# A gated sum of linear attention and a GEGLU block: all gate/up phases ahead of all down phases, and another opening

## The chip, the cores and the metric

The kernel runs on one core of one Trainium2 chip. The metric is device time in microseconds (us) of one execution; three runs of the kernel before gave 289.71, 290.48 and 290.14, a median of 290.14. Engines are named as the profile names them: PE is TensorE (PEld its weight loads), DVE is VectorE, ACT is ScalarE, POOL is GpSimd, SP is SyncE, which here only issues DMAs.

## The reference, cut to what matters

```python
# x: 2048 tokens x 640, bf16; H = 32 heads of Dh = 20; F = 1728
q, k, v = heads(x @ wqkv)
pq, pk  = q @ w_phi[h], k @ w_phi[h]                        # per head, 20 x 20
phi_q   = concat(softmax(pq), softmax(-pq))                 # 40 features a head
phi_k   = concat(softmax(pk), softmax(-pk))
kv, z   = phi_k.T @ v, phi_k.sum(tokens)                    # per head
a = ((phi_q @ kv) / (phi_q @ z + 1e-6)) @ wo                # linear attention, not causal
b = (gelu(x @ w_gate) * (x @ w_up)) @ w_down                # GEGLU block on the same x
g = sigmoid((x * gate_w).sum(-1))
out = g * a + (1 - g) * b
```

`kv` and `z` are sums over all 2048 tokens, so no attention output can be made before the last token has been through `phi_k`. The block `b` depends on `x` alone.

## The kernel before, in words

The program is written out by hand, in the order in which each engine runs it. A small recorder (`_Sched`, L21) notes for each tile which operation wrote it last and which read it, and puts a semaphore wait ahead of an operation that needs one. There is no reordering: what stands first on an engine or a DMA queue runs first, and a wait holds up all that stands behind it on that engine or queue. Two DMA queues are used, SP's and ACT's. A DMA on ACT's queue is issued by ACT itself, between its other instructions.

The 2048 tokens are 16 tiles of 128 rows (index `t`) or four blocks of 512 (index `b`). The 640 columns of x are 5 pieces of 128 (`kt`).

**The opening** (`loads`, L207, and the first half of `attention_state`, L533). SP issues four loads of one tile of x each (`xtok`, L215), the v columns of `wqkv` in three loads (L218), then transposed loads: x tiles 4 and 5 (L227), the k columns of `wqkv` (L222, `wkT`), x tiles 6 and 7, the q columns (`wqT`), x tiles 8 to 11 and 12 to 15, and after those the weights of the second half. ACT first runs one Exp on a constant (L230), which brings its function table in, later one of the four copies of transposed x (L297), then the issues of `wphi` and of the gate's column (L546, L549). PE runs eight matmuls on constants (L539), transposes the four x tiles of the first block (L291), and computes v for these four tiles, one `kt` at a time over all four (`v_step`, L364), so that each load of v columns is used as it lands.

After that come v of tiles 4 and 5, and the folds (`fold`, L319), which multiply the k and q columns by the block-diagonal `w_phi` (matmuls L332, copied out at L345 or L347), five for k and five for q, one for each `kt`. Between them stand v of tiles 6 and 7 (`v_early`) and phi_k's logits of tiles 0 to 3 (`k_early`, both through L352). In the kernel before, all five k folds stand ahead of v of tile 6:

```python
        f(0, "k", (2, 3), "d")
        ...
        f(4, "k", (2, 3), "d")
        ve(6, 4)
        ke(0, 6)
        ve(7, 0)
        ke(1, 2)
```

The pair of numbers is the pair of PSUM banks that a step writes (there are eight, 0 to 7); the letter says whether DVE ("d") or ACT ("a") copies the result out. The logits of tile 3 are made in two pieces, one ahead of the last q fold and one behind it. `k_norm` (L425 to L434, DVE) makes the softmax of phi_k; `gram` (L450) adds one tile to `kv`; `pq` (L512) makes phi_q's exponentials for one block and one piece, with two Exp on ACT (L519). The first three `pq` stand ahead of the first `gram`; they write banks 7, 6 and 0.

**The middle.** For tiles 4 to 15: v and k logits (`vk`), `k_norm`, `gram`, and the remaining `pq`.

**The second half** (`ffn`, L755). For each of the four blocks there is a gate/up phase (`gateups`: 14 chunks of 128 columns of gate and up; gelu on ACT at L628, product on DVE at L630, into the tile `hT`) and a down phase (`downs`: four tiles in two pairs, `down_pair`, L691). The down matmuls (L713) run as 64-row halves side by side. Each adds the product times `w_down` and the attention output times `wo` in one PSUM group; ACT writes it out with the gate's factor (L726), and SP stores it (L737). The step `num` (L646) makes the attention output of one tile: 20 short matmuls (L656), eleven DVE operations (L672 to L685) and one DMA transpose on SP into `goT` (L688). Two `num` stand in the second gate/up phase; the others stand in the down phases, four in each of the first three and two in the last, each well ahead of the pair that uses it. There are two buffers for the product, `hT0` and `hT1`, so a block's gate/up phase cannot be more than two ahead of its down phase:

```python
        gateups(0, state)
        gateups(1, first_nums)
        for b in range(self.NB):
            downs(b, {at[k]: 4 * b + 2 + k for k in range(4 if b < 3 else 2)})
            if b < 2:
                gateups(b + 2, none)
```

## Time and profile before

| | |
|---|---|
| runs | 289.71, 290.48, 290.14 us, median 290.14 |
| profiled execution | 289.71 us, span 288.5 us |
| granted TensorE clock | 1.0 |
| PE busy | 282.2 us (98%), 3018 matmuls |
| DVE busy | 174.7 us (61%) |
| ACT busy | 104.5 us (36%) |
| DMA | 18.67 MB, mean 65 GB/s |
| opening, up to the first `gram` | 0 to 30.9 us |
| middle | 30.9 to 86.7 us |
| gate/up 0 and 1, down 0 | from 86.7 us; down 0 from 141.0 to 162.8 us |
| gate/up 2, down 1 | 162.8 to 192.0 us, 192.0 to 213.8 us |
| gate/up 3, down 2, down 3 | 213.8 to 243.0 us, 243.0 to 264.8 us, from 264.8 us |

The profiled execution is the fastest of the three runs; 1.2 us of its time lie around its span. Durations below are of this execution. A matmul's duration in a row covers its whole way through the array, so matmuls that follow each other overlap: 128x512 has a mean of 379 ns, while one starts every 0.216 us. A few matmul records are missing in the trace (a count of 49 where the program has 50).

### The profile page before, as it was taken

The numbers are of one execution on the slowest core, as the hardware profiler recorded it, in microseconds if no ns is written. First come the engines' busy times: TensorE is split into PE (matmuls) and PEld (weight loads), VectorE is DVE, ScalarE is ACT, GpSimd is POOL, SyncE is SP. The second block draws the span as 40 slices with busy tenths as digits, with TensorE's granted clock in tenths as the row PEclk, the third lists the DMA queues.
The fourth block names the chain that finished last, engine by engine and source line by source line (L and its number), as shares of the span: only waits on it lengthen the run. The fifth ranks groups of instructions, "written<-read, shape, count | busy, mean of one in ns | idle before, by whom it ended". The sixth has DMA issues, their size and how long they took to land.

```text
span 288.5 us, 7003 instructions
## 1 busy us (share of the span) xinstructions
PE 282.2 (98%) x3018; PEld 186.1 (65%) x3033; DVE 174.7 (61%) x353; ACT 104.5 (36%) x199; POOL 5.3 (2%) x36
## 2 busy tenths in 40 slices
PE   8999899999999999999999999999999999999996
PEld 5566589999994444444577544457754445777785
DVE  2337999999987553468588133258823334884801
ACT  3266787776663232322111332311133222112111
POOL 7000000000000000000000000000000000000000
PEclk9999999999999999999999999999999999999999
DMA  6999997000002000011023300003320000222221
GB/s 187 218 190 224 370 368 206 0 2 2 0 2 48 0 0 0 3 24 23 2 25 67 97 0 0 0 3 25 53 89 22 0 0 2 25 49 70 70 72 48
DMA packets 37193, 18.67 MB, mean 65 GB/s; under 512 B 28970, under 2 KB 36906, under 8 KB 37162
## 3 DMA queue, kind: packets, MB, share of 16 engines
q1 hardware_dynamic: 36496, 18.19, 26.4%
q8 instruction: 24, 0.39, 0.5%
q10 hardware_dynamic: 666, 0.03, 0.2%
q14 instruction: 7, 0.06, 0.1%
HBM read 9.04 MB, written 2.62 MB: 40 GB/s over the span
## 4 chain that ended last, share of the span: by engine, by line
PE 94%; DMA 2%; DVE 1%; issue 1%; SPq 1%; ACT 0%; DVEq 0%
PE ps L352 59%; PE ps L713 28%; PE ps L656 2%; PE ps L450 2%; DMA w<-in_A_wqkv_dram 2%; PE ps L364 2%; PE ps L332 1%; SPq L215 1%; DVE Dk L425 1%; DVE wq L345 0%; DVE Ek L434 0%; DVE Dk L429 0%; SPq L218 0%; ACT outsb L726 0%; PE ps L314 0%
## 5 line engine op out<-in xcount | busy, mean ns | idle before, releaser
L630 DVE TENSOR_TENSOR hT<-ps,gl 128x512 bf16<-128x512 f32 x52 | 35.6, 690 | 64.9 <-PE ps L352 64.8
L713 PE MATMUL ps<-wd_sb,hT 64*128 64x320 bf16 (+2 forms) x918 | 66.2, 288 | 0.0
L352 PE MATMUL ps<-xT,wg_sb 128*128 128x512 bf16 (+1 forms) x265 | 63.8, 379 | 0.6 <-issue 0.5
L352 PE MATMUL ps<-xT,wu_sb 128*128 128x512 bf16 (+1 forms) x263 | 63.3, 379 | 0.5 <-DVE hT L630 0.2
L628 ACT ACTIVATE gl<-ps 128x512 bf16<-128x512 f32 x52 | 30.9, 596 | 70.4 <-PE ps L352 66.0
L713 PEld LDWEIGHTS ps<-wd_sb,hT 64*128 64x128 bf16 x918 | 43.1, 94 | 15.6 <-ACT gl L628 0.8
L352 PEld LDWEIGHTS ps<-xT,wu_sb 128*128 128x128 bf16 (+1 forms) x270 | 26.5, 99 | 29.8 <-DVE hT L630 0.5
L352 PEld LDWEIGHTS ps<-xT,wg_sb 128*128 128x128 bf16 (+1 forms) x270 | 26.0, 99 | 29.1 <-issue 0.5
L726 ACT ACTIVATE outsb<-ps,Gm 128x320 bf16<-128x320 f32 (+2 forms) x31 | 14.5, 515 | 75.6 <-PE ps L713 75.6
L352 PE MATMUL ps<-w,xT 128*64 128x512 bf16 (+6 forms) x398 | 41.4, 325 | 0.1
L352 PEld LDWEIGHTS ps<-w,xT 128*64 128x64 bf16 (+1 forms) x400 | 35.7, 107 | 4.7
L713 PE MATMUL ps<-wo_sb,goT 64*128 64x320 bf16 (+2 forms) x340 | 27.8, 288 | 0.0
L352 PE MATMUL ps<-xT,wq 128*64 128x512 bf16 (+1 forms) x184 | 25.9, 380 | 0.1
L434 DVE TENSOR_TENSOR Ek<-Ek,Dk 128x640 bf16<-128x640 bf16 x32 | 25.0, 822 | 0.6
L683 DVE TENSOR_TENSOR O<-ps,RH 128x640 bf16<-128x640 f32 x32 | 24.8, 816 | 0.0
L425 DVE TENSOR_REDUCE Dk<-Ek 128x64 f32<-128x1280 bf16 x16 | 23.7, 1479 | 0.0
L414 ACT ACTIVATE Ek<-ps 128x640 bf16<-128x640 f32 x32 | 20.7, 703 | 4.2 <-PE ps L352 4.2
L519 ACT ACTIVATE Eq<-ps 128x512 bf16<-128x512 f32 x40 | 21.6, 607 | 1.5 <-PE ps L352 1.2
L713 PEld LDWEIGHTS ps<-wo_sb,goT 64*128 64x128 bf16 x340 | 16.0, 94 | 5.4
L352 PEld LDWEIGHTS ps<-xT,wq 128*64 128x64 bf16 (+1 forms) x185 | 15.3, 109 | 2.9
L406 ACT ACTIVATE vaug<-ps 128x640 bf16<-128x640 f32 x12 | 8.5, 706 | 11.5 <-PE ps L352 11.5
L672 DVE RECIPROCAL RH<-ps 128x32 f32<-128x32 f32 x16 | 5.7, 358 | 7.5 <-PE ps L656 6.8
(65 smaller groups left out, 148.9 us busy)
## 6 DMA issues: line engine op xcount, KB each, us to landing
out_dram<-outsb SPq DMA_DIRECT2D x7, 320.0 KB, 2.3
wd_sb<-in_B_w_down_dram SPq DMA_DIRECT2D x1, 2080.0 KB, 13.3
wg_sb<-in_B_w_gate_dram SPq DMA_DIRECT2D x1, 1120.0 KB, 6.3
wu_sb<-in_B_w_up_dram SPq DMA_DIRECT2D x1, 1120.0 KB, 9.6
wg_sb<-in_B_w_gate_dram SPq DMA_DIRECT2D x1, 960.0 KB, 9.5
wu_sb<-in_B_w_up_dram SPq DMA_DIRECT2D x1, 960.0 KB, 9.8
wo_sb<-in_A_wo_dram SPq DMA_DIRECT2D x1, 800.0 KB, 9.8
xtok<-in_A_x_dram SPq DMA_DIRECT2D x4, 160.0 KB, 2.6
```

Of the source, the lines that this page charges most:

```text
L352: self.sc.op("pe", lambda e: e.matmul(self.ps[a:z, bank * 512 + c0:bank * 512 + c0 + n], lhs[:, a:z], rhs, start=first, stop=fin), reads=r ...
L364: sc.op("pe", lambda e, c0=c0, n=n, bk=bk, col=col: e.matmul(self.bank(bk)[:, col:col + n], self.xT[:, kt, t * P:(t + 1) * P], self.w3[:, ...
L406: self.sc.op("act", lambda e: e.activation(self.vaug[:, sv, :, 0:self.DH], self.bank(B, self.D).rearrange("p (h d) -> p h d", d=self.DH), ...
L414: self.sc.op("act", lambda e, s=s, scale=scale: e.activation(self.Ek[:, se, s, :], self.ps[:, o:o + self.D], AF.Exp, scale=scale), reads=[ ...
L425: sc.op("dve", lambda e: e.tensor_reduce(self.Dk[:, se, 0, :].rearrange("p (s h) -> p s h", h=H), self.Ek[:, se, :, :].rearrange("p s (h d ...
L434: sc.op("dve", lambda e, v=v, r=r: e.tensor_tensor(v, v, r, ALU.mult), reads=[("Rk", se)], writes=[("Ek", se, s)])
L519: sc.op("act", lambda e, s=s, scale=scale: e.activation(self.Eq[:, s, i, b * self.BT:(b + 1) * self.BT], self.bank(bank), AF.Exp, scale=sc ...
L628: sc.op("act", lambda e: e.activation(self.gl[:, slot, :], self.bank(banks[0]), AF.Gelu_apprx_tanh), reads=[("ps", banks[0])], writes=[("g ...
L630: sc.op("dve", lambda e: e.tensor_tensor(hT[:, c, :], self.bank(banks[1]), self.gl[:, slot, :], ALU.mult), reads=[("ps", banks[1]), ("gl", ...
L683: dve(lambda e, o=o, f=f, s=s: e.tensor_tensor(o, V[s][:, :, :, 0:DH], f, ALU.mult), rb + [key(6 + s)], [("O", s, sl)], guard=old)
L713: sc.op("pe", lambda e: e.matmul(self.bank(bk, w), lhs, rhs, start=opens and x == 0, stop=end and not opens, skip_group_check=True), reads ...
L726: sc.op("act", lambda e: e.activation(dst, self.bank(bk, w), AF.Copy, scale=g), reads=rd, writes=wr)
```

## The change: the order of the phases, and another opening

In the second half, a third product buffer `hT2` is added, and the product of block 3 is written over the part of `xT` that holds x of blocks 0 to 2, which by then has been read for the last time. So all four gate/up phases run first, and then the four down phases one after the other. The `num` steps keep their places inside their phases.

In the opening, x of the first block comes in two loads of two tiles each, one on SP's queue and one on ACT's; `wphi` and the gate's column follow on ACT's queue at once. The v columns come in five loads of one `kt` each. The Exp at the head of ACT's program is gone, so its table load stands ahead of its first copy. PE's first matmuls are seven on a tile that DVE sets to zero. The copy of x tile 3 moves from DVE to ACT. v of tile 6 moves ahead of the last three k folds, v of tile 7 behind them and ahead of the first k logits, k logits of tiles 1 and 2 move, those of tile 3 are one piece behind the last q fold, and some of the steps use other banks; the third `pq` writes bank 7 and not bank 0.

```diff
+        self.zero = T("zero", [P, 512], BF16)
+        self.hT2 = T("hT2", [P, NFC, BT], BF16)
...
         def xload(q, j):
-            sc.dma(q, lambda e: e.dma_start(self.xtok[:, j, :], x4[:, j, :]), writes=[("xtok", j)])
...
+            sc.dma(q, lambda e: e.dma_start(self.xtok[:, j:j + 2, :], x4[:, j:j + 2, :]),
+                   writes=[("xtok", j), ("xtok", j + 1)])
...
         sc.op("pool", lambda e: e.memset(self.gz[:, :], 0.0), writes=["gz"])
-        sc.op("act", lambda e: e.activation(self.gtmp[:, 0:1], self.nc.const_aps.tensor(1.0, [P, 1], BF16), AF.Exp),
-              writes=["gtmp"])
-        for j in range(self.TB):
-            xload("sp", j)
-        for a, z in ((0, 1), (1, 3), (3, 5)):
-            vload("sp", a, z)
+        xload("sp", 0)
+        xload("act", 2)
+        sc.dma("act", lambda e: e.dma_start(
+            self.wphi_sb[:, :, :], self.wphi.rearrange("h d f -> (h d) f").rearrange("(i p) f -> p i f", p=P)),
+            writes=["wphi"])
+        for kt in range(KD):
+            sc.dma("sp", lambda e: e.dma_start(self.w3[:, kt, 0:D], w3[:, kt, 2 * D:3 * D]), writes=[("wv", kt)])
+        sc.dma("act", lambda e: e.dma_start(self.gz[0:KD, :], self.gw.rearrange("(k p) -> k p", p=P)), writes=["gz"])
         xturn(4, 2)
-        wload(self.wkT, D, "wkT", 0, 5)
+        wload(self.wkT, D, "wkT")
         xturn(6, 2)
...
-        bank = 6 + n % 2 if bank is None else bank
+        bank = 6 + n % 2
...
-        for n in (512, 512, 512, 512, 512, 512, 128, 128):
-            sc.op("pe", lambda e: e.matmul(self.bank(0, n), ones[:, 0:P], ones[:, 0:n], start=True, stop=True),
-                  writes=[("ps", 0)])
+        sc.op("dve", lambda e: e.memset(self.zero[:, :], 0.0), writes=["zero"])
...
+        warm(7)
         xt(0, 6, "d")
         xt(1, 7, "a")
         xt(2, 2, "d")
-        xt(3, 3, "d")
...
+        xt(3, 3, "a")
...
-        ve(4, 6)
-        ve(5, 0)
+        self.v_early(4, 6)
+        self.v_early(5, 0)
         f(0, "k", (2, 3), "d")
         f(1, "k", (4, 5), "a")
-        f(2, "k", (6, 7), "d")
-        f(3, "k", (0, 1), "a")
-        f(4, "k", (2, 3), "d")
-        ve(6, 4)
-        ke(0, 6)
-        ve(7, 0)
-        ke(1, 2)
+        self.v_early(6, 6)
+        f(2, "k", (2, 3), "d")
+        f(3, "k", (4, 5), "a")
+        f(4, "k", (0, 1), "d")
+        self.v_early(7, 6)
+        self.k_early(0, 2)
         f(0, "q", (4, 5), "d")
         f(1, "q", (6, 7), "d")
-        ke(2, 0)
+        self.k_early(1, 0)
         f(2, "q", (4, 5), "d")
         f(3, "q", (6, 7), "d")
-        self.proj(3, 640, 384, 2, 128, ["wk2"])
+        self.k_early(2, 2)
         f(4, "q", (4, 5), "d")
-        self.proj(3, 1024, 257, 3, 0, ["wk2", "wgate"])
-        self.k_evac(3, 2)
         self.k_norm(0)
+        self.k_early(3, 0)
         self.k_norm(1)
         self.pq(0, 1, 1)
         self.pq(0, 0, 0)
-        self.pq(0, 3, 3, 0)
+        self.pq(0, 3, 3)
...
+    def hT(self, b, c):
+
+        if b == 3:
+            return self.xT[:, c // 3, (c % 3) * self.BT:(c % 3 + 1) * self.BT]
+        return (self.hT0, self.hT1, self.hT2)[b][:, c, :]
...
-        oldw, hT = (self.oldw, self.hT0) if b % 2 == 0 else (self.oldk, self.hT1)
-        hk = b % 2
+        old = (self.oldw, self.oldk, [], [("xT", t) for t in range(12)])[b]
+        hT, hk = self.hT(b, c), b
...
         gateups(0, state)
         gateups(1, first_nums)
+        gateups(2, none)
+        gateups(3, none)
         for b in range(self.NB):
             downs(b, {at[k]: 4 * b + 2 + k for k in range(4 if b < 3 else 2)})
-            if b < 2:
-                gateups(b + 2, none)
```

## The prediction

> **What bounds the kernel now.** I read the busy shares and the chain first, then PE's waits behind the opening, then the opening in order of time.
>
> ```profile
> PE 282.2 (98%) x3018; PEld 186.1 (65%) x3033; DVE 174.7 (61%) x353; ACT 104.5 (36%) x199; POOL 5.3 (2%) x36
> PE 94%; DMA 2%; DVE 1%; issue 1%; SPq 1%; ACT 0%; DVEq 0%
> ```
>
> ```profile
> PE ps L450 <- DVE Ek L434: 0.8, 1, 0.8
> PE ps L352 <- issue: 0.5, 3, 0.2
> PE ps L352 <- DVE hT L630: 0.2, 1, 0.2
> ```
>
> The first fence shows a PE-bound kernel. The second lists every wait of PE from 31 us to 288: the 0.8 at its head is the first gram, and behind it lie 0.7 us. So no phase of the second half waits for a buffer, and a third one has no wait to remove. What can move the time is the opening, and the cost of changing from one kind of matmul to another.
>
> ```profile
> 0.84 2.93 PE L539 MATMUL ps<-const-bfloat16-1.0 128*128 128x512 bf16 x8 [0.84 <-PEq L829]
> 3.56 1.81 PE L291 MATMUL ps<-ident,xtok 128*128 128x128 bf16 x15
> 5.63 0.72 PE L291 MATMUL ps<-ident,xtok 128*128 128x128 bf16 x5 [0.26 <-DMA xtok<-in_A_x_dram]
> 6.14 1.36 PE L364 MATMUL ps<-w,xT 128*128 128x480 bf16 x8
> 7.93 3.45 PE L364 MATMUL ps<-w,xT 128*128 128x480 bf16 x24 [0.43 <-DMA w<-in_A_wqkv_dram]
> 15.09 1.96 PE L332 MATMUL ps<-BD,wkT 128*128 128x140 bf16 x30
> 17.09 5.39 PE L352 MATMUL ps<-w,xT 128*128 128x512 bf16 x39
> 22.32 0.79 PE L332 MATMUL ps<-BD,wqT 128*128 128x140 bf16 x12
> 26.87 3.18 PE L352 MATMUL ps<-xT,wq 128*128 128x512 bf16 x14
> 30.88 0.46 PE L450 MATMUL ps<-Ek,vaug 128*64 128x120 bf16 x11 [0.82 <-DVE Ek L434]
> ```
>
> In the timeline of PE (start, length, group, idle before), PE waits for loads of x and v until 7.93 us, then only at the first gram. That wait ends a DVE series:
>
> ```profile
> 24.90 2.30 DVE L345 CAST wq<-ps 128x640 bf16<-128x640 f32 x3 [0.44 <-PE ps L332]
> 27.12 1.48 DVE L425 TENSOR_REDUCE Dk<-Ek 128x64 f32<-128x1280 bf16 x1
> 28.63 0.55 DVE L429 RECIPROCAL Dk<-Dk 128x64 f32<-128x64 f32 x1
> 29.21 1.56 DVE L434 TENSOR_TENSOR Ek<-Ek,Dk 128x640 bf16<-128x640 bf16 x2
> ```
>
> The transposed loads of x tiles 4 and 5 (issued at 4.13) and tiles 6 and 7 (issued at 11.33) took 6.8 and 5.4 us from issue to landing, in this order:
>
> ```profile
> xT<-in_A_x_dram SPq DMA_TRANSPOSE x1, 6.8
> xT<-in_A_x_dram SPq DMA_TRANSPOSE x1, 5.4
> ```
>
> So tiles 6 and 7 landed at 16.73. Their first use, v of tile 6, began at 16.88 (its shown start, 17.09, less one missing record of 0.216): they were 0.15 us early, by luck of the order.
>
> **The change, part by part.** Parts 1 to 3 lead to the first gram, part 4 is the rest.
>
> *1. First loads.* Both x loads are issued at 0.80 now; before, the fourth was issued at 2.19 and landed 3.4 later, at 5.6. 0.66 MB at the 261 GB/s of the window from 2 to 5 us need 2.5 us; with first packets at about 2.0, x lands at 4.5 at best. At worst it lands at 5.6, as before. I take 5.0, the middle, since nothing shows two queues at once. DVE's memset of zeros is bounded by POOL's 128x128 memset (0.20) and a DVE copy of 128x640 (0.49); seven warm-up matmuls at 0.42 (eight, or 6.5 lengths of 512, filled 0.84 to 3.56) end at about 4.1: hidden under the x loads, and if x came earlier they would cost up to 0.6. ACT issues three DMAs (0.41, 0.43, 0.66) and loads its table (1.28) by 3.7, 2 us ahead of its first copy: nothing, unless x came before 3.5. `wphi` lands earlier, and nothing waited for it on the chain.
>
> The 20 transposes took 0.107 each. The warm-up matmuls of 128x512 have a mean of 626 ns, later ones 379: PE runs at half speed until some 6.4 us, although the granted clock reads 1.0 throughout. From 5.0, 13 transposes fit before 6.4, seven more at half the time end at 6.8. ACT copies x tile 1 and then tile 3 at 0.70 each, where DVE took 0.49, so tile 3 is ready at 7.7; the last v pair (0.27) ends the first `kt` at 8.0, against 7.93 before. Each v load is one `kt` now: the second lands between 6.0 (the first one before) and 7.85 (the double one), so nothing waits. Opening: +0.1, between -0.3 (x at 4.5) and +1.6.
>
> The +1.6 is what stays cold: if half speed lasted until 9.8, the transposes would end at 7.1 and the first `kt` at 9.5. The Trainium skill, "TensorE: Matmul & The Clock Gate", Part 1, says the clock opens after a busy window of about 3.4 us that runs free of the kernel; PE now idles from 4.1 to 5.0, so one more window is possible. By this estimate from the page, the whole sum below would be +0.4 instead of -0.1; no row here shows the window.
>
> *2. v of tile 6, moved ahead of three k folds.* Each fold has six matmuls. The 12 of two q folds filled 22.32 to 22.95: 0.63. So v of tile 6 is reached at 15.09 + 0.63 = 15.72, +0.1: 15.8. The tiles land at 16.73 if nothing changes. SP reaches their issue about 0.5 us earlier (six issues at 0.46 instead of seven), which would give 16.2. But the DMA share is 0.91 to 1.24 in all windows from 2 to 17 us; the engines, not SP, look full, and the bytes ahead are the same. I take 16.73: a new wait of 0.9 us, in which PE does nothing, and which swallows any delay of part 1 below 0.9. Bounds: 16.2, and 18.1 if this load takes the 6.8 of its sister. What queues behind: all of PE. The k and q columns (landed 14.0 and 20.2) stay ahead of their use at 15.2 and 21.8.
>
> *3. From there to the first gram.* A v step or a k step takes 1.36 (four filled 16.88 to 22.32). v6, three k folds (0.95), v7, k0, two q folds (0.63), k1, two q folds, k2, one q fold (0.32): 9.33, then k3: 10.69, two `pq` of 1.08: 12.85. The third `pq` writes bank 7, as the first did, so it waits for ACT: k3's exponentials occupied ACT for 1.23 (26.92 to 28.15) from 0.26 after PE, until 12.2; the first `pq`'s two Exp finish at 13.3. A new wait of 0.5; the third `pq` ends at 14.4. DVE copies the last q fold by 10.3 and needs 3.57 (27.12 to 30.69): 13.9, earlier than PE. So the old 0.82 wait is gone and a bank wait stands there. The first gram starts at 16.73 + 14.4 = 31.15, against 30.88: +0.3. With the bounds of part 2: -0.25 and +1.6. From there every row is PE's again, so this passes to the end.
>
> *4. Order of phases.* PE's work is the same. Two rows show the change from down to gate/up:
>
> ```profile
> 162.98 1.03 PE L352 MATMUL ps<-xT,wg_sb 128*128 128x512 bf16 x4 [0.16 <-issue]
> 214.00 1.03 PE L352 MATMUL ps<-xT,wg_sb 128*128 128x512 bf16 x4 [0.16 <-issue]
> 140.23 0.81 PE L352 MATMUL ps<-xT,wu_sb 128*128 128x512 bf16 x3
> 140.98 0.31 PE L713 MATMUL ps<-wd_sb,hT 64*128 64x320 bf16 x2
> ```
>
> In the last two, three matmuls from 140.23 at 0.216 end their issue at 140.88; the down matmul follows 0.10 later. Two changes each way go: 4 x 0.10 = 0.4. Bounds: 0, if the array drains elsewhere, and 0.5 with the idle column's 0.16. Product writes over `xT` wait for PE's reads of the third phase, past already; if not, one DVE product (0.69). The down phases stand back to back, as down 2 and 3 did: DVE was busy 16.15 of 21.72 us there, and PE did not wait. The transposed attention output of the last `num` has 57 steps of 0.133, plus 14, or 9.4 us, for 0.4 on PE, 4.0 on DVE (a quarter of 16.15) and 2.8 of DMA. On SP each transpose still stands behind the same store. Nothing.
>
> Sum: +0.3 - 0.4 = -0.1 on the profiled 289.71 (span 288.5 and 1.2 around it). That execution is 0.43 below the median, so I forecast 290.0 against 290.14.
>
> **The rivals.**
> *A. Slower: tiles 6 and 7 land later.* ACT's queue now sends `wphi`, 640 short rows, into the v loads, and the sister load took 6.8. Against it: same bytes. Landing at 18.1 instead of 16.73 gives 290.0 + 1.4 = 291.4; it decides from 17.75 on, when the total passes +0.87.
> *B. Faster: loads are bound by SP's issue.* Tiles land 0.5 earlier, and the first gram comes 0.55 earlier than in the sum: 289.5. To pass 0.87 the tiles must be there by 16.0; in full, with x at 4.5, PE reaches tile 6 at 15.4 and finds it: first gram at 29.8, -1.1, with -0.4: 288.6. For it speaks SP's unbroken series of issues; against it the full DMA share.
> *C. The third buffer does nothing at all* (changes cost PE the same elsewhere): +0.3, 290.4. *D. Half speed lasts one window longer:* PE reaches tile 6 at 17.2, 0.5 later than in the sum: 290.5. Both are inside the band below.
>
> **How the numbers follow.** 0.3%, or 0.87 us, is about what a measurement of this kernel can tell from no change. Forecast with C, D and B's milder form: 0.50. A, with any other late load in the opening: 0.36. B in full: 0.14. Range: 289.1 to 291.4; its top is A's price, its lower end lies between B's 289.5 and 288.6, and some 2 in 10 stay outside. The forecast's own range is 289.3 to 290.9.
>
> **What would show it.** Right: an idle time of PE of about 0.9 ahead of v of tile 6, put down to `xT`'s load; about 0.5 ahead of the third `pq`, put down to ACT; none ahead of the first gram, at about 31.2; one change to the down matmuls instead of three, and no new wait of PE behind 31 us. Wrong: tiles 6 and 7 outside 16.2 to 17.7, or a wait inside the run of four down phases.

## The result, and the profile after

The changed kernel takes 288.37 us (median of 6 runs, 287.87 to 289.37), the kernel before beside it 289.74 (6 runs, 289.20 to 290.48). The ratio is 0.9954, with a 95% interval of 0.9933 to 0.9976: 1.3 us or 0.46% faster. The forecast was 290.0, in a range from 289.1 to 291.4. The profiled execution took 288.19 us, its span 286.9.

The page's busy shares and its chain of the changed kernel read almost as before:

```profile
PE 281.2 (98%) x3017; PEld 185.5 (65%) x3032; DVE 174.7 (61%) x353; ACT 105.0 (37%) x199; POOL 5.3 (2%) x36
PE 93%; SPq 3%; DMA 2%; ACT 1%; issue 1%; ACTq 0%
```

PE's work is the same, so the gain lies in when PE could begin it. The waits of PE from 31 us on, of the changed kernel:

```profile
PE ps L352 <- DVE hT L632: 0.2, 1, 0.2
PE ps L352 <- issue: 0.2, 1, 0.2
```

The wait at the first gram is gone, and of three issue waits of 0.5 in all one of 0.2 is left. The opening, in the timeline of PE of the changed kernel (start, length, group, idle before):

```profile
1.24 3.17 PE L541 MATMUL ps<-zero 128*128 128x512 bf16 x7 [1.24 <-DVE zero L537]
4.29 1.29 PE L291 MATMUL ps<-ident,xtok 128*128 128x128 bf16 x20
5.42 4.72 PE L364 MATMUL ps<-w,xT 128*128 128x480 bf16 x32
...
13.84 0.79 PE L332 MATMUL ps<-BD,wkT 128*128 128x140 bf16 x12
14.80 1.53 PE L352 MATMUL ps<-w,xT 128*128 128x512 bf16 x10 [0.18 <-DMA xT<-in_A_x_dram]
16.18 1.11 PE L332 MATMUL ps<-BD,wkT 128*128 128x140 bf16 x18
...
25.90 2.11 PE L352 MATMUL ps<-xT,wq 128*128 128x512 bf16 x9
28.34 1.25 PE L352 MATMUL ps<-xT,wq 128*128 128x512 bf16 x5 [0.34 <-ACT Eq L519]
29.52 0.48 PE L450 MATMUL ps<-Ek,vaug 128*64 128x120 bf16 x11
```

The 20 transposes start at 4.29, all 32 matmuls of the first four `kt` of v follow without a pause (before, the second `kt` began at 7.93), v of tile 6 waits 0.18, and the first gram starts at 29.52 instead of 30.88: 1.36 us earlier. On DVE the softmax is ready ahead of it (27.43 + 1.56 = 28.99):

```profile
25.33 1.47 DVE L425 TENSOR_REDUCE Dk<-Ek 128x64 f32<-128x1280 bf16 x1
27.43 1.56 DVE L434 TENSOR_TENSOR Ek<-Ek,Dk 128x640 bf16<-128x640 bf16 x2
```

Behind the first gram this pair of profiles shows little: up to the first gate/up matmul 49.27 us against 49.24 (it starts at 80.12 in the kernel before, since some gate/up chunks already stand in the middle), from there to PE's last start 205.08 against 205.51 (-0.43), and from that to the end of the span 3.06 against 2.84 (+0.2). The phases are in the order meant, with one change to down matmuls (timeline of PE, changed kernel):

```profile
196.97 1.03 PE L352 MATMUL ps<-xT,wu_sb 128*128 128x512 bf16 x4
197.93 0.31 PE L714 MATMUL ps<-wd_sb,hT 64*128 64x320 bf16 x2
198.07 0.56 PE L658 MATMUL ps<-KV,Eq 64*128 64x88 bf16 x20
```

So in this pair -1.36 belong to the opening. What moved there are the loads. The timeline of SP's queue (issue and how long SP was held by it), of the changed kernel:

```profile
0.79 0.41 SPq L217 DMA_DIRECT2D xtok<-in_A_x_dram  x1
1.27 2.30 SPq L234 DMA_DIRECT2D w<-in_A_wqkv_dram  x5
3.62 1.44 SPq L225 DMA_TRANSPOSE xT<-in_A_x_dram  x1
5.10 4.58 SPq L221 DMA_TRANSPOSE wkT<-in_A_wqkv_dram  x1
9.72 1.41 SPq L225 DMA_TRANSPOSE xT<-in_A_x_dram  x1
```

and of the kernel before:

```profile
0.80 1.83 SPq L215 DMA_DIRECT2D xtok<-in_A_x_dram  x4
2.67 1.42 SPq L218 DMA_DIRECT2D w<-in_A_wqkv_dram  x3
4.13 2.25 SPq L227 DMA_TRANSPOSE xT<-in_A_x_dram  x1
6.43 4.87 SPq L222 DMA_TRANSPOSE wkT<-in_A_wqkv_dram  x1
11.33 1.40 SPq L227 DMA_TRANSPOSE xT<-in_A_x_dram  x1
```

x tiles 6 and 7 are issued at 9.72 instead of 11.33 and land 5.0 later instead of 5.4,

```profile
xT<-in_A_x_dram SPq DMA_TRANSPOSE x1, 5.0
```

that is at 14.72 instead of 16.73. Of these 2.01 us, 0.51 is the earlier start of the first transposed load (3.62, 4.13), 0.81 and 0.29 are that the two transposed loads ahead hold SP for 1.44 and 4.58 instead of 2.25 and 4.87, and 0.4 is the landing. In the window from 2 to 5 us (length, busy time and count of PE, PEld, DVE, ACT and POOL, granted clock, DMA share, GB/s) the kernel before shows

```profile
2.00:5.00 3.00, 3.00 (x20) 2.03 (x19) 0.49 (x1) 0.41 (x3) 2.29 (x15) 1.00 0.91 261
```

and the changed kernel

```profile
2.00:5.00 3.00, 3.00 (x19) 1.32 (x18) 0.22 (x1) 1.28 (x1) 2.29 (x15) 1.00 1.03 324
```

A share of 0.91 stood beside 261 GB/s, one of 1.03 beside 324: the share of 0.91 was no ceiling.

### The profile page after: what moved, and what is told of

Read it like the earlier page. It is cut to its first block, busy times and chain, and to the rows that moved or that the text cites. A ratio compares the mean times of both kernels' runs of the same rounds, so it can differ in the third digit from the quotient of the medians.

```text
span 286.9 us, 7006 instructions
## 1 busy us (share of the span) xinstructions
PE 281.2 (98%) x3017; PEld 185.5 (65%) x3032; DVE 174.7 (61%) x353; ACT 105.0 (37%) x199; POOL 5.3 (2%) x36
## 4 chain that ended last, share of the span: by engine, by line
PE 93%; SPq 3%; DMA 2%; ACT 1%; issue 1%; ACTq 0%
PE ps L352 60%; PE ps L714 28%; PE ps L658 2%; DMA xT<-in_A_x_dram 2%; PE ps L450 2%; SPq L221 2%; PE ps L332 1%; SPq L234 1%; SPq L225 1%; ACT Ek L414 0%; ACT Eq L519 0%; SPq L217 0%; ACT outsb L727 0%; ACT gcol L417 0%; ACTq L42 0%
## 5 line engine op out<-in xcount | busy, mean ns | idle before, releaser
L632 DVE TENSOR_TENSOR hT<-ps,gl 128x512 bf16<-128x512 f32 x39 | 26.7, 690 | 38.6 <-PE ps L352 38.5
L714 PE MATMUL ps<-wd_sb,hT 64*128 64x320 bf16 x648 | 49.5, 296 | 0.0
L352 PEld LDWEIGHTS ps<-xT,wu_sb 128*128 128x128 bf16 (+1 forms) x270 | 26.5, 99 | 29.8 <-DVE hT L632 0.5
L714 PEld LDWEIGHTS ps<-wd_sb,hT 64*128 64x128 bf16 x648 | 31.0, 94 | 12.1 <-issue 0.4
L632 DVE TENSOR_TENSOR xT<-ps,gl 128x512 bf16<-128x512 f32 x13 | 9.0, 691 | 18.2 <-PE ps L352 18.2
L714 PE MATMUL ps<-wd_sb,xT 64*128 64x320 bf16 (+2 forms) x270 | 16.7, 269 | 0.0
```

Source lines behind the costliest of these rows:

```text
L352: self.sc.op("pe", lambda e: e.matmul(self.ps[a:z, bank * 512 + c0:bank * 512 + c0 + n], lhs[:, a:z], rhs, start=first, stop=fin), reads=r ...
L632: sc.op("dve", lambda e: e.tensor_tensor(hT, self.bank(banks[1]), self.gl[:, slot, :], ALU.mult), reads=[("ps", banks[1]), ("gl", slot)], ...
L714: sc.op("pe", lambda e: e.matmul(self.bank(bk, w), lhs, rhs, start=opens and x == 0, stop=end and not opens, skip_group_check=True), reads ...
```

## The experiments

Each is told by its edit to the kernel before or to the changed kernel. Kernels of one group ran on one chip, with runs of the kernel before on that chip. Its medians lie between 289.66 and 290.82, so only ratios and differences within a group are compared. A word on single profiles: the same kernel's first gram differs between executions (29.52 and 30.31 in two profiles of the changed kernel), so the profiles carry places and waits, and the runs carry the time.

### First group: the change taken apart (kernel before: 289.66)

**The order of phases alone**, on the kernel before:

```diff
+        self.hT2 = T("hT2", [P, NFC, BT], BF16)
...
         gateups(1, first_nums)
+        gateups(2, none)
+        gateups(3, none)
         for b in range(self.NB):
             downs(b, {at[k]: 4 * b + 2 + k for k in range(4 if b < 3 else 2)})
-            if b < 2:
-                gateups(b + 2, none)
```

> The kernel before with only the third product buffer and the new order of the phases. Theory 1 (the opening made most of the gain, the order of phases the predicted 0.4): 0.4 us faster than before, first gram at 30.9 as before, one change from gate/up to down matmuls instead of three. Theory 2 (the order of phases made the gain): 1.2 us or more faster. Rival (nothing comes of it): within 0.1.

Measured: 289.49, ratio 0.999 (0.9978 to 1.0002), about 0.3 us at the ratio. The runs alone do not tell it from nothing. The profiles do: from the start of the first gram to the end of the span, the nine profiles here that have the new order of phases show 256.90 to 257.42, mean 257.16; the eleven that have the old one show 257.20 to 257.80, mean 257.55. The order of phases is worth 0.39. From the first gate/up matmul to PE's last start, which leaves out both ends, the two sets don't even touch: 204.91 to 205.08 with the new order, 205.34 to 205.51 with the old one.

**The changed kernel with the old order of phases**, the same edit the other way:

```diff
-        gateups(2, none)
-        gateups(3, none)
         for b in range(self.NB):
             downs(b, {at[k]: 4 * b + 2 + k for k in range(4 if b < 3 else 2)})
+            if b < 2:
+                gateups(b + 2, none)
```

> The changed kernel with the second half put back to the old order (two buffers in use). Theory 1: about 1.0 us faster than before, first gram at 29.5; with the 0.4 of the phases this gives the whole. Theory 2: within 0.2 of before.

Measured: 288.65, ratio 0.9963 (0.9949 to 0.9977), -1.0 by medians; first gram at 29.42. The opening carries the gain of the first gram whole, and the two halves (-0.3 and -1.07 at their ratios) add up to the change.

**The loads alone**, on the kernel before, with its order of folds and steps:

```diff
-        for j in range(self.TB):
-            xload("sp", j)
-        for a, z in ((0, 1), (1, 3), (3, 5)):
+        xload("sp", 0)                       # two tiles each
+        xload("act", 2)
+        ...                                  # wphi and the gate's column on ACT's queue
+        for a, z in ((0, 1), (1, 2), (2, 3), (3, 4), (4, 5)):
             vload("sp", a, z)
```

The Exp on a constant is left out of this one as well.

> The kernel before with only the loads of the opening changed: x in two loads on two queues, w_phi and the gate's column on ACT's queue behind it, v columns in five loads, no Exp ahead; PE's order and warm-up stay. Theory 1a (the loads carry the opening's gain): x on hand at about 4.3, v of tile 6 about 1.2 us earlier than 16.88 without a wait, 0.8 to 1.2 us faster than before. Theory 1b (the order of the folds carries it, the loads only feed it): less than 0.4, since the DVE series ahead of the first gram stays.

Measured: median 288.94, ratio 0.9987 (0.9962 to 1.0012). The interval is wide because the executions fall into two bands: eight from 288.43 to 289.04, four from 290.85 to 291.33. The profile is of the lower band (timeline of PE, loads alone):

```profile
4.29 1.29 PE L294 MATMUL ps<-ident,xtok 128*128 128x128 bf16 x20 [0.52 <-DMA xtok<-in_A_x_dram]
5.42 4.67 PE L367 MATMUL ps<-w,xT 128*128 128x480 bf16 x32
29.57 0.46 PE L453 MATMUL ps<-Ek,vaug 128*64 128x120 bf16 x11 [0.82 <-DVE Ek L437]
```

With the old folds, and with the old wait of 0.82 still there, the first gram comes at 29.57. In the lower band (median 288.71, 0.95 faster) the loads give nearly the whole gain of the opening; the new order of folds and steps adds 0.05 to the first gram (29.52).

**The new order of folds and steps alone**, with their banks, on the kernel before:

```diff
-        f(2, "k", (6, 7), "d")
-        f(3, "k", (0, 1), "a")
-        f(4, "k", (2, 3), "d")
-        ve(6, 4)
+        self.v_early(6, 6)
+        f(2, "k", (2, 3), "d")
+        f(3, "k", (4, 5), "a")
+        f(4, "k", (0, 1), "d")
...
-        self.pq(0, 3, 3, 0)
+        self.pq(0, 3, 3)
```

> The kernel before with only the new order of folds, v and k steps and their banks; loads stay. By the prediction's parts 2 and 3: tiles 6 and 7 land at 16.7, PE waits 0.9 for them, first gram at 31.15, 0.3 us slower than before. Theory 1b: faster by 0.4 or more.

Measured: 290.37, ratio 1.0023 (1.0008 to 1.0038), 0.7 us slower. Timeline of PE, folds alone:

```profile
14.84 0.79 PE L332 MATMUL ps<-BD,wkT 128*128 128x140 bf16 x12
16.48 1.53 PE L352 MATMUL ps<-w,xT 128*128 128x512 bf16 x10 [0.85 <-DMA xT<-in_A_x_dram]
...
29.91 1.25 PE L352 MATMUL ps<-xT,wq 128*128 128x512 bf16 x5 [0.34 <-ACT Eq L519]
31.10 0.49 PE L450 MATMUL ps<-Ek,vaug 128*64 128x120 bf16 x11
```

This is the picture that the prediction drew for the whole change: 0.85 ahead of v of tile 6 (forecast 0.9), 0.34 ahead of the third `pq` (0.5), no wait at the first gram, which comes at 31.10 (31.15). With the old loads its parts 2 and 3 hold.

### Second group: what of the loads (kernel before: 290.82)

**Both x loads on SP**, in the loads-alone kernel:

```diff
-        xload("act", 2)
+        xload("sp", 2)
```

> The loads-only kernel with both x pairs on SP's queue. Theory 1a' (longer rows carry the gain): x as early as with two queues or up to 0.5 later (second issue at 1.26), span within 0.4 of the loads-only kernel's 287.2. Theory 1a'' (the second queue carries it): x at 5 or later, span near the 288.5 of before.

Measured: 289.41, ratio 0.9955 (0.9937 to 0.9972). x lands in two steps (transposes from 3.71, the second half at about 5.0), the first `kt` of v waits 0.61, the second starts at 7.46, and the window from 2 to 5 us moves 292 GB/s. With the first gram at 30.39 the profile looks as if the second queue were needed, but the runs don't bear that out: they are 1.3 us faster at the ratio, as the changed kernel's were, and within 0.2 of the two-queue kernel with the longer warm-up below, on the same chip. Two double loads hold SP for 0.88 us, four single ones for 1.83, two on two queues for 0.41; the first halving is enough to keep the gain.

**Four single x loads, two on each queue**, in the loads-alone kernel:

```diff
-        xload("sp", 0)
-        xload("act", 2)
+        for q, js in (("sp", (0, 1)), ("act", (2, 3))):
+            for j in js:
+                xload(q, j)                  # one tile each
```

> The loads-only kernel with four one-tile x loads, two on each queue. Theory 1a' (longer rows): x lands at 5 or later although two queues issue it, 261 GB/s or so between 2 and 5 us. Theory 1a'' (the second queue): x at 4.3 to 4.6 and the rate stays near 324 GB/s.

Measured: 288.90, ratio 0.9937 (0.9915 to 0.9959); the second `kt` at 6.78, 318 GB/s from 2 to 5 us. The loads are as short as in the kernel before, and the rate is nearly that of the changed kernel: longer loads are not needed for it. That the second queue raised it above the 292 of one queue rests on one profile each; SP is held by its x issues for 0.89 here, as with both pairs on one queue.

**A longer warm-up**, eight matmuls of 512 columns, in the loads-alone kernel:

```diff
-        for n in (512, 512, 512, 512, 512, 512, 128, 128):
+        for n in (512,) * 8:
```

> The loads-only kernel with eight full warm-up matmuls, so that PE works until x is there. Theory 3 (a pause of PE ahead of the transposes lets the full speed come a window later in some executions, which makes the loads-only kernel's runs of 290.9 to 291.3): no run over 290, median 288.6, like the opening of the changed kernel. Rival (those runs have another cause, loads that come late): a quarter to a third of the runs stay at 290.9 or more.

Measured: 289.26, ratio 0.9951 (0.9933 to 0.9968); all six executions between 288.74 and 289.75, and PE idles 0.18 ahead of the transposes instead of 0.52. There is no second band, but with a third of the executions in it, six without one come about by chance in 9 of 100 cases ((2/3)^6), and the chip is another.

**The changed kernel with its third `pq` back in bank 0:**

```diff
-        self.pq(0, 3, 3)
+        self.pq(0, 3, 3, 0)
```

> The changed kernel with the third pq in bank 0 again. Theory 4 (the wait of 0.34 us ahead of the third pq is ACT's hold on bank 7 and lies on the path): the wait goes, first gram 0.3 to 0.4 earlier at about 29.1, 0.3 us faster than the changed kernel. Rival: the DVE series ends last then (29.0 in the changed kernel) and leaves less than 0.1.

Measured: 288.04, ratio 0.9906 (0.9885 to 0.9926). From 5 us on the profile shows no wait of PE at all.

### Third group: bank 0 beside the changed kernel, and two single parts (kernel before: 289.99)

The changed kernel itself once more, and the bank-0 form beside it:

> The changed kernel itself, beside the next run on the same chip: 288.2 to 288.8 if this chip is like the first, 1.0 to 1.5 us faster than before.

> The changed kernel with the third pq in bank 0, now beside the changed kernel on one chip. Theory 4: 0.3 us faster than the changed kernel (its wait was 0.34). Rival: within 0.1 of it.

Measured: 288.38, ratio 0.9941 (0.9920 to 0.9961), and 287.74, ratio 0.9915 (0.9894 to 0.9936). The profile of the changed kernel is of its slowest execution here (288.76). In the timeline of PE:

```profile
6.69 4.69 PE L364 MATMUL ps<-w,xT 128*128 128x480 bf16 x32
15.70 1.52 PE L352 MATMUL ps<-w,xT 128*128 128x512 bf16 x10
30.31 0.49 PE L450 MATMUL ps<-Ek,vaug 128*64 128x120 bf16 x11
```

PE comes to v of tile 6 only at 15.70 and does not wait, for tiles 6 and 7, issued at 9.43, landed at 14.2.

By medians bank 0 is 0.64 faster than the changed kernel; by means 0.74, give or take 0.4. The profiles show how much of it is the bank: from the start of v of tile 6 to the first gram it takes 14.60 to 14.72 in the eight profiles that have the new order of steps and the third `pq` in bank 7, and 14.17 in both with bank 0. So the bank is worth about 0.44, a little more than the idle time of 0.34 that it removes; the rest of the 0.64 is within the noise. The timeline of PE of the bank-0 form, where the 0.34 of the changed kernel stood:

```profile
14.59 1.52 PE L352 MATMUL ps<-w,xT 128*128 128x512 bf16 x10
25.35 3.40 PE L352 MATMUL ps<-xT,wq 128*128 128x512 bf16 x15
28.76 0.46 PE L450 MATMUL ps<-Ek,vaug 128*64 128x120 bf16 x11
```

Three `pq` in a row and the gram behind them, with no wait. This is the fastest version: it beats both kernels, 2.25 us ahead of the one before on this chip.

**Only x in two loads on two queues**, on the kernel before, without the Exp; v stays in three loads, `wphi` and the gate's column late:

```diff
-        for j in range(self.TB):
-            xload("sp", j)
+        xload("sp", 0)
+        xload("act", 2)
```

> The kernel before with only x of the first block in two loads on two queues (and without the Exp, which would hold up ACT's issue); v columns in three loads and w_phi late, as before. Theory 1 in its narrowest form (the early x carries the opening's gain): x on hand at about 4.3, 0.7 us or more faster than before. Rival (the v columns in five loads or the early w_phi are needed too): PE waits for v columns up to 7.4 or so, less than 0.4 faster.

Measured: 293.39, ratio 1.0098 (1.0059 to 1.0137), 3 us slower. Timeline of PE, x alone:

```profile
6.55 5.67 PE L363 MATMUL ps<-w,xT 128*128 128x480 bf16 x32
14.28 0.23 PE L313 MATMUL ps<-ident,gz 128*128 128x128 bf16 x1 [2.05 <-DMA gz<-in_gate_w_dram]
```

With SP's issues ahead of time, the transposed load of the k columns is issued at 4.73, and `wphi`, issued on ACT's queue at 5.74, lands only 8.6 us later (4.0 in the changed kernel, where it is issued at 1.24). PE stands 2.05 us ahead of the gate's column, which is issued behind `wphi`, and then the granted clock falls. Windows of the same kernel, columns as above, the granted clock third from the end:

```profile
14.00:15.00 1.00, 0.72 (x6) 0.50 (x7) 0.63 (x3) 0.25 (x1) 0.00 (x0) 1.00 1.15 240
15.00:16.00 1.00, 0.83 (x6) 0.30 (x4) 1.00 (x5) 1.00 (x3) 0.00 (x0) 0.72 0.90 105
16.00:17.00 1.00, 1.00 (x3) 0.29 (x2) 0.99 (x3) 0.33 (x1) 0.00 (x0) 0.50 1.09 195
17.00:18.00 1.00, 1.00 (x5) 0.42 (x4) 0.00 (x0) 0.00 (x0) 0.00 (x0) 0.50 1.28 290
18.00:19.00 1.00, 1.00 (x8) 0.67 (x7) 0.00 (x0) 0.30 (x1) 0.00 (x0) 0.57 1.02 230
```

The lost clock is (0.28 + 0.50 + 0.50 + 0.43) = 1.7 us more. Four of the six executions show a mean clock of 0.994, which over 290 us is the same 1.7; they took 292.87 to 294.35, the other two 290.86 and 291.65.

**The changed kernel without its seven warm-up matmuls**, whose product nothing reads:

```diff
-        warm(7)
```

> The changed kernel without its seven warm-up matmuls. Theory 3 (half speed until some 3.4 us or more of steady work): transposes and the first v steps at half speed, 20 transposes in 2.1 instead of 1.1 us, first gram 1 to 2.5 us later, 1 to 2.5 us slower than the changed kernel. Rival (the loads alone set the opening): within 0.3 of it.

Measured: 289.57, ratio 0.9988 (0.9968 to 1.0008), 1.2 slower than the changed kernel beside it. Timeline of PE:

```profile
4.66 2.32 PE L291 MATMUL ps<-ident,xtok 128*128 128x128 bf16 x20 [4.66 <-POOL hmask L277]
6.77 6.13 PE L364 MATMUL ps<-w,xT 128*128 128x480 bf16 x32
```

The transposes and the first v steps run at half speed (6.77 - 4.66 = 2.11 for 20 transposes, 1.13 in the changed kernel). The warm-up is what lets PE use loads that come early.

### Fourth group (kernel before: 290.43)

**The loads-alone kernel with v in three loads:**

```diff
-        for a, z in ((0, 1), (1, 2), (2, 3), (3, 4), (4, 5)):
+        for a, z in ((0, 1), (1, 3), (3, 5)):
```

> The loads-only kernel with the v columns in three loads again, so the x-only kernel plus the early w_phi and gate column. Theory 5 (in the x-only kernel the late w_phi and gate column alone made the loss, queued behind the transposed loads that now start earlier): no wait ahead of the gate column, no second spell at half speed, like the loads-only kernel, near 288.5 in its quicker runs. Rival (five loads of v are needed too): PE waits for v columns after the first kt, 0.4 or more slower than the loads-only kernel.

Measured: 290.42, ratio 0.9985 (0.9958 to 1.0012), again in two bands, 288.73 to 290.04 and 290.80 to 291.29, five each. Timeline of PE:

```profile
5.88 1.31 PE L367 MATMUL ps<-w,xT 128*128 128x480 bf16 x8
8.04 3.45 PE L367 MATMUL ps<-w,xT 128*128 128x480 bf16 x24 [0.86 <-DMA w<-in_A_wqkv_dram]
```

PE waits 0.86 for the second piece of v; the first gram comes at 30.99. The wait for the gate's column, of the x-alone kernel, is not there: early `wphi` removes that.

**Only `wphi` and the gate's column early**, on the kernel before, without the Exp:

```diff
-        sc.op("act", lambda e: e.activation(self.gtmp[:, 0:1], ..., AF.Exp), writes=["gtmp"])
...
+        sc.dma("act", lambda e: e.dma_start(self.wphi_sb[:, :, :], ...), writes=["wphi"])
+        sc.dma("act", lambda e: e.dma_start(self.gz[0:self.KD, :], ...), writes=["gz"])
...                                          # the two late issues go
```

> The kernel before with only the early issue of w_phi and the gate column on ACT (and without the Exp); x in four loads on SP and v in three as before. Theory 1 (the second queue for x carries the gain): within 0.3 of before, first gram near 30.9. Rival (getting the short rows out of the way of the transposed loads carries it): tiles 6 and 7 land 0.5 or more earlier, 0.5 or more faster.

Measured: 289.83, ratio 0.9978 (0.9958 to 0.9997): 0.6 faster by medians. Its profile does not show why: x waits 0.96, the second `kt` starts at 8.22 and the first gram at 31.16, all later than in the profile of the kernel before, and tiles 6 and 7 land at 16.7, as before. So this gain rests on the interval alone, whose end is near 1, and the Exp that is left out has a part in it that was not measured by itself.

### Fifth group (kernel before: 290.33)

**Only v in five loads**, on the kernel before:

```diff
-        for a, z in ((0, 1), (1, 3), (3, 5)):
+        for a, z in ((0, 1), (1, 2), (2, 3), (3, 4), (4, 5)):
```

> The kernel before with only the v columns in five loads of one kt each. Theory 6 (the double load of the second and third kt is what holds PE up; alone it lands earlier): no wait or at most 0.3 ahead of the second kt, which starts at 6.9 to 7.4 instead of 7.9 to 8.3; first gram at 30.0 to 30.5, 0.4 to 0.9 us faster than before. Rival (x early on two queues is needed): second kt at 7.7 or later, within 0.3 of before.

Measured: 289.61, ratio 0.9967 (0.9949 to 0.9985), 0.7 faster. The second `kt` starts at 7.13 instead of 7.93; from there v of tile 6 runs into its load (0.63), and the first gram comes at 30.64.

**The changed kernel with v in three loads**, the same edit the other way:

> The changed kernel with the v columns in three loads again. Theory 6: the wait of 0.4 to 0.9 ahead of the second kt comes back, second kt at about 8.0, first gram at 30.6 or later, 1 us slower than the changed kernel, near 289.3. Rival (x and w_phi carry the gain): within 0.3 of the changed kernel's 288.4.

Measured: 289.05, ratio 0.9957 (0.9940 to 0.9975). It keeps most of the gain by the runs: five loads are worth something by themselves, but the changed kernel doesn't hang on them. The expected wait ahead of the second `kt` did not come: it starts at 7.62 without one. The profiled execution was the slowest of the nine (290.09); PE waits 1.37 in it, ahead of v of tile 6.

### Sixth group (kernel before: 290.18)

**The changed kernel with x in four loads on SP:**

```diff
-        xload("sp", 0)
-        xload("act", 2)
+        for j in range(self.TB):
+            xload("sp", j)
```

> The changed kernel with x of the first block in four loads on SP's queue again; w_phi and the gate's column stay early on ACT, v in five loads. Theory 7 (no single edit of the loads carries the opening; any two of them do): 0.9 to 1.4 us faster than before, as the changed kernel. Rival (x on two queues carries it): 0.6 faster or less.

Measured: 290.24, ratio 1.0009 (0.9984 to 1.0034). The gain is gone by the median, with seven executions from 289.30 to 290.25 (their median 0.5 faster than the kernel before) and five from 291.50 to 292.25. The timeline of PE shows the forecast's wait again, larger:

```profile
14.74 0.79 PE L331 MATMUL ps<-BD,wkT 128*128 128x140 bf16 x12
17.19 1.53 PE L351 MATMUL ps<-w,xT 128*128 128x512 bf16 x10 [1.66 <-DMA xT<-in_A_x_dram]
```

x tiles 6 and 7 are issued at 11.70, and the window from 2 to 5 us moves 210 GB/s. Four of the five executions of the upper band have the mean clock of 0.994 of the x-alone kernel; the profile is of the lower band, so a fall of the clock behind this wait is likely there and not shown. What is taken away here is not the second queue alone: x goes back to four issues, which hold SP for 1.83. Two double loads on the one queue kept the gain (second group), though beside the old order of folds.

**The changed kernel with `wphi` and the gate's column issued late**, where the kernel before issues them:

> The changed kernel with w_phi and the gate's column issued late on ACT again, behind its copies of x. Theory 8 (with early loads the late issue falls behind the transposed loads): w_phi lands after 11, PE waits ahead of the gate's column, 1 us or more slower than the changed kernel. Rival: it lands by 10 and the kernel stays within 0.3 of the changed one.

Measured: 289.27, ratio 0.9967 (0.9946 to 0.9989), in two bands, 288.62 to 288.92 and 289.62 to 290.59, six each. The profiled execution is of the upper band (290.58) and shows the place:

```profile
12.84 0.23 PE L310 MATMUL ps<-ident,gz 128*128 128x128 bf16 x1 [1.20 <-DMA gz<-in_gate_w_dram]
```

The first gram comes at 31.98, 2.5 us behind that of the changed kernel's first profile. The wait explains 1.2 of it; the transposes also ran at half speed throughout in this execution, and the first v step began at 6.96 instead of 5.42. In the lower band the kernel is as fast as the changed one against its own chip (288.67 - 290.18 = -1.5). So early `wphi` is a cover against a wait that comes in some executions; that it is the wait which parts the two bands is not shown, since no profile of the lower band was had.

## Why the prediction was wrong, by its own steps

**The step that failed** is in part 2, "I take 16.73": that x tiles 6 and 7 land as before, since "the engines, not SP, look full, and the bytes ahead are the same". They landed at 14.72, and in the second profile of the changed kernel at 14.2. The share of busy DMA engines was read as a ceiling; the same engines moved 324 GB/s in a window where they had moved 261. In the profiles, the window from 2 to 5 us showed 210 to 265 with four single x loads on SP, 284 to 292 with two queues and v in three loads, 292 with two pairs on SP and v in five, and 302 to 332 with two queues and v in five loads. The 0.5 of SP's earlier issues, which the prediction worked out and then set aside, was measured as 0.51; the other 1.5 were not foreseen at all.

What made the load early can be read from the issues of tiles 6 and 7 in the profiles:

| x of the first block | v columns | issued | landed | profiles |
|---|---|---|---|---|
| four loads on SP | three loads | 11.05 to 11.62 | 16.4 to 17.0 | 4 |
| four loads on SP | five loads | 11.11, 11.70 | 16.6, 17.2 | 2 |
| two loads on two queues | three loads | 10.92 to 11.73 | 15.7 to 16.9 | 3 |
| two loads on two queues | five loads | 9.26 to 9.85 | 13.7 to 15.2 | 9 |
| two double loads on SP | five loads | 10.04 | 14.9 | 1 |
| four single loads, two on each queue | five loads | 10.52 | 16.4 | 1 |

Neither fewer x loads on SP nor five loads of v brings the issue forward by much alone; both together do, by some 1.5 to 2 us with two queues, and by about 1 without the second queue. The difference lies in how long SP is held from the start of the first transposed load to the issue of tiles 6 and 7. In pairs that differ by the v loads alone this falls from 8.2 to 5.7 (loads alone), from 8.1 to 5.7 or 6.1 (changed kernel) and from 7.2 to 6.1 (kernel before) when three loads become five. With four x loads, the five issues of v then cost SP 0.9 more, which uses up most of that. Why SP is held for a shorter time behind smaller v loads is not shown, and all rows but the first and the fourth rest on few profiles. The changed kernel with v in three loads keeps most of its gain by the runs, and its profile is of its slowest execution, so the third row can't hold for all of them.

**Part 1** failed in two terms in the first profile of the changed kernel, and there partly by luck. The two loads of x landed at 4.3 and 4.4, where 4.5 was given as the best: that was worked out from the 261 GB/s of before, with four issues in a row. And the transposes ran at full speed from the start, so they took 1.13 instead of 1.8; the first v step began at 5.42 and not at 6.8. Together PE came to tile 6 at 14.47 (13.84 and 0.63 for two folds) instead of 15.8. In the second profile both terms stood close to the forecast: x landed at 4.6 and 4.8 (forecast 5.0), only the last 6 of the 20 transposes ran at full speed, the first v step began at 6.69 and v of tile 6 at 15.70. Its first gram, at 30.31, is earlier than the forecast 31.15 by the load of tiles 6 and 7 alone. The early loads and the warm-up both count (without warm-up +1.2). That the second `kt` of v would not wait was right.

**Parts 2 and 3**, the waits that the new order makes, were right where the loads are the old ones: 0.85 against 0.9 and 0.34 against 0.5. That the first gram comes out so well there (folds alone, 31.10 against 31.15) is in part luck: v of tile 6 began 0.25 earlier than forecast, and what follows took 14.62 instead of 14.4. In the first profile of the changed kernel the wait of 0.9 shrank to 0.18, because both sides moved: PE came 1.3 earlier than forecast, the load 2.0. In the second it is gone. The bank-7 wait of 0.34 stayed, and from v of tile 6 to the first gram it took 14.6 to 14.7.

**Part 4** was right in mechanism and size: 0.4 forecast, 0.43 in the pair of profiles behind the first gate/up matmul, 0.39 over twenty profiles from the first gram to the end. No wait appeared in the run of four down phases. That the third buffer would remove no wait was right too: there was none.

**Rival B** is nearest to what happened, in its full form: x at 4.5 and PE at tile 6 at 15.4 were to give a first gram at 29.8 and 288.6; measured were 4.4, 14.47, 29.52 and 288.37. It was given 0.14, and what spoke for it, SP's unbroken series of issues, was the sounder reading of the two. That its time comes out so close has some luck in it: the cause that it gives was worth 0.5 at the tiles, its full form takes them as landed by 15.4 without a term for that, and it started from a median of 290.14 for the kernel before, which became 289.74 with the six runs. That 0.40 is part of the miss of the forecast's 290.0 as well, and no step of the prediction made it. **Rival A** did not come: with `wphi` among them the v loads took 3.7 to 4.7 us from issue to landing (before, 3.3 for the one of the same size and 5.0 for the double ones), and the tiles behind them landed earlier, not later. It is a late `wphi` that costs, up to 2.05 of waiting. **Rival C** is refuted by the twenty profiles. **Rival D** did not show in the two profiles of the changed kernel: PE came to tile 6 at 14.47 and 15.70, not at 17.2.

A page bears on the failed step. The Trainium skill, "DMA: Bandwidth & Descriptors", section "Issuing engines are not separate DMA queues", says that starting DMAs from several engines saves only the sequencer's time to initiate them, usually small beside the DMA. The time saved here agrees: of the fall from 1.83 us to 0.41 in what x's issues hold SP for, the second queue itself made 0.47 (0.88 with both pairs on SP), small beside a load of 3.5; the rest comes from making two loads out of four. But with v in five loads the series of transposed loads behind moved forward by more than was saved, by 1.61 us at the issue of tiles 6 and 7.

**What stays open** is how the gain in time divides among the loads. Alone, v in five loads gives 0.7, early `wphi` some 0.6 at an interval that nearly reaches 1, x on two queues loses 3. Four single x loads on SP cost the changed kernel its whole gain; the other two edits, taken from it, cost less than the runs can tell with certainty. The parts work together: x on two queues with v in three loads has the long transposed load of the k columns issued at 4.73, ahead of a late `wphi`, which then lands late. Nor is it shown what the upper band of the loads-alone kernel is. Its mean granted clock is 0.999 to 1.0, so it is not the clock's fall of the x-alone kernel. A later start of full speed is not ruled out by that: the kernel without warm-up ran its transposes and first v steps at half speed, and its mean clock reads 1.0 as well. No profile of such an execution was had.

## What to carry to other kernels

A DMA share near 1 was no sign here that no more bytes could be moved (0.91 beside 261 GB/s, 1.03 beside 324): before taking a landing time as fixed, add up what the issuing queue is held by, and ask when each later load could be issued if the first ones left it sooner. When a change brings loads forward, recount every load that is issued late and every bank that is shared behind it, for they are the next to be waited for: here a 25 KB load on the other queue, and a bank whose return to 0 gave some 0.4 to 0.6 us more. Steps that a forecast costs against the old landing times should be costed against the new ones as well, since an order that loses 0.7 with the old loads cost nothing with the new (first gram at 29.52, and at 29.57 with the old order). And an edit that does little alone can be half of one that does much: fewer x loads on SP and v in five loads brought tiles 6 and 7 forward only together.

## What was not expected of the hardware

In the x-alone kernel, a pause of PE of about 2 us in the midst of full-speed work was followed, a microsecond after it ended, by some 3.4 us at half the granted clock (0.72, 0.50, 0.50, 0.57 in the windows above). The profile shows it in one execution; by the mean clock of 0.994 it came in four of six. The Trainium skill, "TensorE: Matmul & The Clock Gate", Part 1, gives an idle window of about 3.4 us for this and calls the window free-running; here a pause shorter than that was enough, and the half-speed stretch has about that length.

At the start, however, the clock's column reads 1.0 while the matmuls run at half speed. In the traces of the two kernels the record of the clock begins only at 6.37 us (before) and at 4.30 (changed), where the matmuls come to full speed, and the views count time without a record as 1.0. The two kernels' transposes, by line and form (min, median and max in ns), first of the kernel before and then of the changed one:

```profile
L291 PE MATMUL ps<-ident,xtok x20: 290/314/315, 3.6 to 6.0; 128*128 128x128 bf16 x20
```

```profile
L291 PE MATMUL ps<-ident,xtok x20: 219/219/230, 4.3 to 5.4; 128*128 128x128 bf16 x20
```

So in the first microseconds speed is read from the durations and not from the clock's column.
